# Output stores of 32, 64 or 96 rows in a kernel that fuses a Fourier mixing layer and a SoLU MLP

## The chip, the cores and the metric

The kernel runs on one core of one Trainium2 chip. The metric is the device time of one execution in microseconds (us).

## What is computed

`x` holds 8 batches of S = 3136 tokens with D = 256 channels. The first half filters along the tokens in the frequency domain, the second half is an MLP with a softmax-weighted activation and a norm. `moe_...` names are passed to the second function without the prefix.

```python
def _attn_ref(x, w_r, w_i, b_r, b_i):
    X = np.fft.rfft(x, axis=1)
    Xr, Xi = X.real, X.imag
    Yr = Xr @ w_r - Xi @ w_i + b_r
    Yi = Xr @ w_i + Xi @ w_r + b_i
    # soft threshold by 0.01 on Yr and Yi
    Y = Yr + 1j * Yi
    return np.fft.irfft(Y, n=x.shape[1], axis=1)

def _moe_ref(x, w_in, w_out, g_ln):     # x: 25088 x 256, w_in: 256 x 1024, w_out: 1024 x 256
    h = x @ w_in
    sm = softmax(h)
    solu = h * sm
    ln = (solu - mean(solu)) / sqrt(var(solu) + 1e-6) * g_ln
    return ln @ w_out
```

## The kernel before, in words

**The transform.** S = 98 x 32: a token has the number n1 * 32 + n2 with n1 below N1 = 98 and n2 below N2 = 32. Forward, `fwd1` does the 98-point part (matmuls with `fa`), its result goes to HBM (`s1`), `fwd2` does the 32-point part (`fb`), `mix` applies the weights and the threshold, `inv1` (`gb`) goes back along the 32 and stores `zout` to HBM (`s2`), the last piece as `zs`. `inv2` does the inverse 98-point part for one group of G2 = 4 values of n2: it loads `zt` from `s2`, and its matmuls with `ia` leave 4 x 98 tokens in a PSUM bank, for each half `eh` of the channels one bank. So the tokens of a batch leave the transform in the order n2, n1, not in that of the output.

**The ring.** ACT casts a bank to float16 (`ring_hi`), DVE writes what the cast lost (`ring_lo`). Both are rings of R = 8 tiles of 128 tokens; a group of 392 tokens that reaches the end of the ring is evicted in two pieces.

**The MLP.** It goes in tiles of 128 tokens of the ring, 49 for a pair of batches. `moe_head` does the first matmul (`ph`, 12 matmuls of 512 columns), the exponentials and sums; `moe_turn` casts the activations to `lh` and `ll`, transposes both by DMA into `th` and `tl` and works out the norm's factor `r`; `moe_tail` does the second matmul (`po`, 16 matmuls with `th`, 8 with `tl`), scales on ACT into `o` (two buffers) and stores it. A tile's rows are consecutive in (n2, n1), so one store can only cover the rows of one n2, whose distance in the output is 32 rows of 1 KB: a tile of 128 rows is cut wherever n2 changes, at places that move from tile to tile. This is the loop at the end of `moe_tail`:

```python
        n2, n1 = divmod(jj, N1)
        n = min(N1 - n1, (t + 1) * P - j)
        nc.sync.dma_start(out_v[2 * bp + bb, n2, n1 : n1 + n], o[p0 : p0 + n])
```

The 25th tile of a pair (t = 24) holds the last 64 tokens of the first batch and the first 64 of the second; `h_scale` makes it a scale factor out of two.

**The order.** Nothing is issued as it is written. Each operation is recorded by `Plan.take` with a key; `Plan.order` then lays all of them out by list scheduling over the five engines with its own durations: it takes, on the engine that can start first, the ready operation with the lowest key, and tile buffers are given out in the order of their first users' keys. `Plan.issue` emits the result, so all instructions carry line 342, and the trace is read by tile names. All DMAs are issued by SP, in that one order. Keys count tiles: tile n of batch b has the key `first + n`; `inv2` of a group has a key 2 below the tile that first needs it; `front_b` (fwd2, mix, inv1 of batch b + 1) has keys that begin at `first` and are spread over the batch's tiles, `front_a` (fwd1 of batch b + 2) at `first + 6`.

Of the kernel before, what the change touches and what calls it, by code (L numbers as in the profile page):

```python
# [15 lines left out]
F16 = mybir.dt.float16  # L16
U32 = mybir.dt.uint32
AF = mybir.ActivationFunctionType
ALU = mybir.AluOpType
# [5 lines left out]
S, N1, N2 = 3136, 98, 32  # L25
# [7 lines left out]
S_SCALE, B_SCALE, Z_SCALE, X_SCALE = 2.0**-7, 2.0**-5, 2.0**-11, 2.0**-11  # L33

LOW = 2.0**11
# [416 lines left out]
def fft_mix_solu_kernel(ctx: ExitStack, tc, x, w_r, w_i, b_r, b_i, w_in, w_out, g_ln, fa, fbf, fsf, iaf, fa16, fb, fs, gb, gs, ia, out):  # L452
    nc = Plan(tc.nc)
    B, _, D = x.shape
    FF = w_in.shape[1]
    P = 128
    ND = D // P
# [5 lines left out]
    out_v = out.rearrange("(b n1 n2) e -> b n2 n1 e", b=B, n1=N1)  # L463
# [4 lines left out]
    fp = Pool(ctx.enter_context(tc.tile_pool(name="fp", bufs=2)), 2)  # L468
# [60 lines left out]
    peaks, scales = {}, {}  # L529
# [132 lines left out]
    NU = Q // 2 + 1  # L662
# [165 lines left out]


    G2 = 4  # L830
    R = 8 * P
    ring_hi = const.tile([P, ND, R], F16, name="ring_hi")
    ring_lo = const.tile([P, ND, R], F16, name="ring_lo")

    def inv2(b, g):
        if b >= PLAIN_Z:
            zt = fp.tile([P, G2, 2, D], F16, name="zt", bufs=2)[:N1]
            nc.sync.dma_start(zt.rearrange("c n t d -> c (n t d)"), s2[b][:, g * G2 * 2 * D : (g + 1) * G2 * 2 * D])
        else:
            zt = fp.tile([P, G2, D], F32, name="zt", bufs=2)[:N1]  # L840
            nc.sync.dma_start(zt.rearrange("c n d -> c (n d)"), s2[b][:, g * G2 * D : (g + 1) * G2 * D])
        j0 = (b * S + g * G2 * N1) % R
        n = G2 * N1
        first = min(n, R - j0)
        for eh in range(ND):
            pa = banks.tile("pf")
            nc.reserve(*(ring[:, eh, to : to + z - a] for ring in (ring_hi, ring_lo) for a, z, to in ((0, first, j0), (first, n, 0)) if z > a))
            with nc.together():
                for i in range(G2):
                    es = slice(eh * P, (eh + 1) * P)  # L850
                    if b < PLAIN_Z:
                        nc.tensor.matmul(pa[:, i * N1 : (i + 1) * N1], zt[:, i, es], iaf_s, start=True, stop=True)
                        continue
                    for k, (t, j) in enumerate(((0, 0), (0, 1), (1, 2))):
                        nc.tensor.matmul(pa[:, i * N1 : (i + 1) * N1], zt[:, i, t, es], ia_s[:, j], start=k == 0, stop=k == 2)
            for a, z, to in ((0, first, j0), (first, n, 0)):
                if a == z:
                    continue
                hi, lo = (ring[:, eh, to : to + z - a] for ring in (ring_hi, ring_lo))
                nc.scalar.activation(hi, pa[:, a:z], AF.Copy, scale=X_SCALE)  # L860
                nc.vector.scalar_tensor_tensor(lo, hi, -LOW, pa[:, a:z], ALU.mult, ALU.add)


    def h_scale(k):

        b0, b1 = (2 * k[0] + (k[1] * P + j) // S for j in (0, P - 1))
        if b0 == b1:
            return scales[b0]["h"]
        hs = sp.tile([P, 1], F32, name="hs", bufs=2)
        half = S % P  # L870
        nc.vector.tensor_copy(hs[:half], scales[b0]["h"][:half])
        nc.vector.tensor_copy(hs[half:], scales[b1]["h"][half:])
        return hs

    def moe_head(k):
        j = (2 * k[0] * S + k[1] * P) % R
        hi, lo = ring_hi[:, :, j : j + P], ring_lo[:, :, j : j + P]
        down = h_scale(k)
        ph, nm = [], []
        for h in range(2):  # L880
            cs = slice(h * HF, (h + 1) * HF)
            p = banks.tile("ph")
            n = 0
            with nc.together():
                for dh in range(ND):
                    for lh, rh in ((hi, win_hi), (hi, win_lo), (lo, win_low)):
                        nc.tensor.matmul(p, lh[:, dh], rh[:, dh, cs], start=n == 0, stop=n == 3 * ND - 1)
                        n += 1
            m = sp.tile([P, 1], F32, name="nm")
            nc.vector.tensor_reduce(m, p, AX.X, ALU.max, negate=True)  # L890
            ph.append(p)
            nm.append(m)
        m = sp.tile([P, 1], F32, name="m")
        nc.vector.tensor_scalar(m, nm[0], nm[1], down, ALU.min, ALU.mult)

        c = sp.tile([P, 1], F32, name="c")
        nc.vector.tensor_scalar(c.bitcast(U32), m.bitcast(U32), 0x7FFFFFFF, None, ALU.bitwise_and)
        nc.vector.tensor_scalar(c, c, 1.0, 2.0**-13, ALU.max, ALU.mult)
        nc.vector.reciprocal(c, c)
        ch = sp.tile([P, 1], F32, name="ch")  # L900
        nc.vector.tensor_scalar(ch, c, down, None, ALU.mult)
        u = mp.tile([P, FF], F32, name="u", bufs=4)
        se = [sp.tile([P, 1], F32, name=f"se{h}") for h in range(2)]
        su = [sp.tile([P, 1], F32, name=f"su{h}") for h in range(2)]
        for h in range(2):
            cs = slice(h * HF, (h + 1) * HF)
            nc.scalar.activation(u[:, cs], ph[h], AF.Exp, bias=m, scale=down, accum_out=se[h])
            nc.vector.scalar_tensor_tensor(u[:, cs], ph[h], ch, u[:, cs], ALU.mult, ALU.mult, accum_out=su[h])


        total = sp.tile([P, 1], F32, name="total")
        nc.gpsimd.tensor_tensor(total, su[0], su[1], op=ALU.add)
        nc.gpsimd.tensor_tensor(se[0], se[0], se[1], op=ALU.add)
        a = sp.tile([P, 1], F32, name="a")
        nc.gpsimd.tensor_scalar(a, se[0], 1e-9, c, ALU.add, ALU.mult)
        nc.gpsimd.tensor_tensor(a, a, a, op=ALU.mult)
        return k, u, total, a
# [21 lines left out]
    def moe_tail(k, parts, r):  # L939
        th, tl = parts  # L940
        po = banks.tile("po")
        n = 0
        for part, halves in ((th, 2), (tl, 1)):
            with nc.together():
                for f in range(NF):
                    for j in range(halves):
                        nc.tensor.matmul(po[:, :D], part[:, f], wout[:, f, j], start=n == 0, stop=n == 3 * NF - 1)
                        n += 1
        o = mp.tile([P, D], F32, name="o", bufs=2)
        nc.scalar.activation(o, po[:, :D], AF.Copy, scale=r)  # L950
        bp, t = k
        j = t * P
        while j < (t + 1) * P:
            bb, jj = divmod(j, S)
            n2, n1 = divmod(jj, N1)
            n = min(N1 - n1, (t + 1) * P - j)
            p0 = j - t * P
            nc.sync.dma_start(out_v[2 * bp + bb, n2, n1 : n1 + n], o[p0 : p0 + n])
            j += n

# [168 lines left out]
    def front_b(b, key, step):  # L1131

        lag = 4 if b == 0 else 3
        for n in range(NU + lag):
            nc.key = key + n * step
            for fn, u in ((fwd2, n), (mix, n - 1)):
                if 0 <= u < NU:
                    fn(b, u)
            u = n - lag
            if u == NU - 1 or 0 <= u < NU and b == 0:  # L1140

                inv1(b, u, u + 1)
            elif 0 < u < NU and u % 2:
                inv1(b, u - 1, u + 1)
# [18 lines left out]
    heads, turned = [], []  # L1163
    first = 0
    for b in range(B):
        tiles = range(0, 24) if b % 2 == 0 else range(24, 49)
        L = len(tiles)
        if b == 0:
            front_a(1, -40, 0.5)
        if b + 2 < B:  # L1170
            front_a(b + 2, first + 6, (L - 6) / 17)
        if b + 1 < B:
            front_b(b + 1, first + (6 if b == 0 else 0), (L - (8 if b == 0 else 2)) / (NU + 3))
        groups = 0
        for n, t in enumerate(tiles):
            need = min((t + 1) * P - (b % 2) * S, S)
            while groups < N2 // G2 and groups * G2 * N1 < need:
                nc.key = first + n - 2
                inv2(b, groups)
                groups += 1  # L1180
            nc.key = first + n
            heads.append(moe_head((b // 2, t)))
            nc.key = first + n + 0.5
            turned.append(moe_turn(*heads.pop(0)))
            nc.key = first + n + 1
            moe_tail(*turned.pop(0))
        while groups < N2 // G2:
            inv2(b, groups)
            groups += 1
        first += L  # L1190
    nc.issue(tc)

# [23 lines left out]
```

## Time and profile before

| | us |
|---|---|
| median of 3 runs (lowest, highest) | 1635.44 (1632.08, 1636.81) |
| the profiled execution | 1638.51 |
| its span on the core | 1636.7 |
| PE matmul busy | 1586.2 |
| DVE, ACT, POOL busy | 1317.3, 1234.6, 1129.3 |
| mean granted TensorE clock | 0.986 |

The profile shows one execution. Engines: PE matmuls, PEld weight loads beside them, DVE, ACT, POOL; SPq is SP's queue, which issues the DMAs. Idle time before an instruction is put down to what released it, as `<-DMA th<-lh`: the transposing DMA that writes `th` from `lh`. A DMA's own row on SPq is the time of its issue, not of its transfer.

### The profile page before, as it was taken

The numbers are of one execution on the slowest core, as the hardware profiler recorded it, in microseconds if no ns is written. First come the engines' busy times: TensorE is split into PE (matmuls) and PEld (weight loads), VectorE is DVE, ScalarE is ACT, GpSimd is POOL, SyncE is SP. The second block draws the span as 40 slices with busy tenths as digits, with TensorE's granted clock in tenths as the row PEclk, the third lists the DMA queues.
The fourth block names the chain that finished last, engine by engine and source line by source line (L and its number), as shares of the span: only waits on it lengthen the run. The fifth ranks groups of instructions, "written<-read, shape, count | busy, mean of one in ns | idle before, by whom it ended". The sixth has DMA issues, their size and how long they took to land.

```text
span 1636.7 us, 37871 instructions
## 1 busy us (share of the span) xinstructions
PE 1586.2 (97%) x13040; PEld 1127.8 (69%) x13040; DVE 1317.3 (80%) x3343; ACT 1234.6 (75%) x2496; POOL 1129.3 (69%) x1889
## 2 busy tenths in 40 slices
PE   6979999999999999999999999999999999999998
PEld 3545877676775787668766677766877677676675
DVE  4778779985888867997799977899689877777774
ACT  4667678885788767887678867788678876678786
POOL 0656777676875687768766687766887677776775
PEclk8989999999999999999999999999999999999999
DMA  8868966997669977899758996699767977669776
GB/s 249 274 223 205 194 149 155 229 207 146 151 151 233 214 152 133 189 249 192 162 102 191 251 209 132 134 234 243 162 134 158 191 165 145 119 137 144 150 130 106
DMA packets 532258, 290.23 MB, mean 177 GB/s; under 512 B 425978, under 2 KB 502300, under 8 KB 532064
## 3 DMA queue, kind: packets, MB, share of 16 engines
q1 hardware_dynamic: 532064, 287.81, 80.9%
q8 instruction: 102, 1.67, 0.4%
q14 instruction: 92, 0.75, 0.1%
HBM read 107.89 MB, written 77.07 MB: 113 GB/s over the span
## 4 chain that ended last, share of the span: by engine, by line
PE 78%; DMA 8%; DVE 5%; ACT 3%; POOL 2%; issue 2%; SPq 0%; DVEq 0%; ACTq 0%; POOLq 0%
PE po L342 26%; PE ph L342 24%; PE pf L342 23%; PE pb L342 4%; DMA th<-lh 4%; DMA tl<-ll 3%; DVE u L342 1%; POOL ll L342 1%; ACT junk L342 1%; DVE xl L342 1%; ACT lh L342 1%; DVE nm L342 1%; ACT u L342 0%; DMA zt<-s 0%; DVE av L342 0%
## 5 line engine op out<-in xcount | busy, mean ns | idle before, releaser
L342 POOL TENSOR_TENSOR ll<-u,lh 128x1024 f16<-128x1024 f32 x196 | 427.2, 2180 | 116.0 <-ACT lh L342 110.0
L342 PE MATMUL po<-wout,th 128*128 128x256 f16 x3136 | 375.3, 273 | 10.6 <-DMA th<-lh 9.2
L342 PEld LDWEIGHTS <-th 128*128 128x128 f16 x3136 | 303.8, 98 | 74.5 <-DMA th<-lh 15.8
L342 ACT ACTIVATE u<-ph,m,hsb 128x512 f32<-128x512 f32 x384 | 296.1, 776 | 50.5 <-DVE m L342 46.9
L342 DVE TENSOR_REDUCE nm<-ph 128x1 f32<-128x512 f32 x392 | 265.0, 684 | 82.3 <-PE ph L342 80.7
L342 DVE SCALAR_TENSOR_TENSOR u<-ph,ch,u 128x512 f32<-128x512 f32 x392 | 281.6, 747 | 31.1 <-ACT u L342 20.0
L342 PE MATMUL ph<-win_hi,ring_hi 128*128 128x512 f16 x784 | 298.2, 380 | 1.3 <-DVE ring_lo L342 0.8
L342 PE MATMUL ph<-win_low,ring_lo 128*128 128x512 f16 x784 | 297.8, 380 | 0.0
L342 PE MATMUL ph<-win_lo,ring_hi 128*128 128x512 f16 x784 | 297.8, 380 | 0.0
L342 ACT CAST lh<-u 128x1024 f16<-128x1024 f32 x196 | 205.3, 1047 | 64.2 <-DVE u L342 57.2
L342 PEld LDWEIGHTS <-ring_hi 128*128 128x128 f16 x1568 | 150.3, 98 | 142.7 <-issue 5.9
L342 ACT ACTIVATE junk<-u,total 128x1024 bf16<-128x1024 f32 x196 | 226.0, 1153 | 13.1 <-POOL total L342 12.8
L342 PE MATMUL po<-wout,tl 128*128 128x256 f16 x1568 | 204.2, 273 | 6.3 <-DMA tl<-ll 6.3
L342 PEld LDWEIGHTS <-tl 128*128 128x128 f16 x1568 | 150.4, 98 | 39.8 <-DMA tl<-ll 8.6
L342 POOL TENSOR_TENSOR y<-yt,yc 128x512 f32<-128x512 f32 (+1 forms) x104 | 133.0, 1279 | 61.0 <-ACT yt L342 32.7
L342 POOL TENSOR_TENSOR yl<-y,yh 128x512 f16<-128x512 f32 (+1 forms) x104 | 127.2, 1224 | 47.6 <-ACT yh L342 47.0
L342 PE MATMUL pf<-w_hi,Xh 128*128 128x256 f16 (+1 forms) x546 | 149.2, 273 | 0.0
L342 PE MATMUL pf<-w_hi,Xl 128*128 128x256 f16 (+1 forms) x546 | 148.8, 273 | 0.0
L342 PE MATMUL pf<-w_lo,Xh 128*128 128x256 f16 (+1 forms) x546 | 148.8, 273 | 0.0
L342 ACT ACTIVATE o<-po,r 128x256 f32<-128x256 f32 x196 | 92.6, 473 | 72.0 <-PE po L342 53.8
L342 PEld LDWEIGHTS <-ring_lo 128*128 128x128 f16 x784 | 76.7, 98 | 93.8 <-DVE ring_lo L342 0.8
L342 PEld LDWEIGHTS <-Xh 128*128 128x128 f16 (+1 forms) x1196 | 114.2, 99 | 27.7 <-issue 3.7
(189 smaller groups left out, 2851.0 us busy)
## 6 DMA issues: line engine op xcount, KB each, us to landing
xt<-in_x_dram SPq DMA_DIRECT2D x108, 392.0 KB
zt<-s SPq DMA_DIRECT2D x56, 392.0 KB
s<-zout SPq DMA_DIRECT2D x42, 512.0 KB
s<-av SPq DMA_DIRECT2D x48, 392.0 KB
bin<-s SPq DMA_DIRECT2D x36, 512.0 KB
out_dram<-o SPq DMA_DIRECT2D x64, 98.0 KB
bin<-s1f SPq DMA_DIRECT2D x12, 512.0 KB
s1f<-av SPq DMA_DIRECT2D x10, 392.0 KB
```

Source lines behind the costliest of these rows:

```text
L342: getattr(engine, name)(*args, **kw)
```

## The change

A tile now takes tokens of 96-token runs: for each n2 the ring gets the first N96 = 96 of the 98 tokens, so a batch has 24 tiles of 128 = 96 + 32, 64 + 64 or 32 + 96 rows. The last two tokens of each n2, 64 for a batch, go to a tile of their own, `last_hi` and `last_lo`, one buffer each, that two batches fill; it is the pair's 25th tile of the second batch (t is None), and in the output its rows are two runs of 64. The ring has R = 2 x 4 x 96 tokens, two groups; a bank is evicted into the ring and into `last` by two instructions on each engine. `front_b` of batches 2 to 7 begins two keys earlier, with a smaller step, and `inv2` of a group stands 3 keys below the tile that needs it.

```diff
     G2 = 4
-    R = 8 * P
+    N96 = N1 - N1 % 16
+    R = 2 * G2 * N96
...
-        j0 = (b * S + g * G2 * N1) % R
-        n = G2 * N1
-        first = min(n, R - j0)
+        j0 = (b * N2 + g * G2) * N96 % R
+        if g == 0 and b % 2 == 0:
+            lasts[b // 2] = [fp.tile([P, ND, 2, N1 - N96, N2], F16, name=f"last_{part}", bufs=1) for part in ("hi", "lo")]
...
+            to = [
+                (
+                    ring[:, eh, j0 : j0 + G2 * N96].rearrange("p (i n) -> p i n", n=N96),
+                    last[:, eh, b % 2, :, g * G2 : (g + 1) * G2].rearrange("p n i -> p i n"),
+                )
+                for ring, last in zip((ring_hi, ring_lo), lasts[b // 2])
+            ]
+            nc.reserve(*to[0], *to[1])
...
-            for a, z, to in ((0, first, j0), (first, n, 0)):
-                if a == z:
-                    continue
-                hi, lo = (ring[:, eh, to : to + z - a] for ring in (ring_hi, ring_lo))
-                nc.scalar.activation(hi, pa[:, a:z], AF.Copy, scale=X_SCALE)
-                nc.vector.scalar_tensor_tensor(lo, hi, -LOW, pa[:, a:z], ALU.mult, ALU.add)
+            pv = pa[:, : G2 * N1].rearrange("p (i n) -> p i n", n=N1)
+            for hi, lo, ns in zip(*to, (slice(0, N96), slice(N96, N1))):
+                nc.scalar.activation(hi, pv[:, :, ns], AF.Copy, scale=X_SCALE)
+                nc.vector.scalar_tensor_tensor(lo, hi, -LOW, pv[:, :, ns], ALU.mult, ALU.add)
...
     def moe_head(k):
+        b, t = k
+        if t is None:
+            hi, lo = (part.rearrange("p e b n i -> p e (b n i)") for part in lasts.pop(b // 2))
+        else:
+            j = (b * N2 * N96 + t * P) % R
...
+        b, t = k
+        if t is None:
+            for i in range(2):
+                nc.sync.dma_start(out[(b + i) * S - P // 2 : (b + i) * S], o[i * P // 2 : (i + 1) * P // 2])
+            return
+        p = 0
+        while p < P:
+            n2, n1 = divmod(t * P + p, N96)
+            n = min(N96 - n1, P - p)
+            nc.sync.dma_start(out_v[b, n2, n1 : n1 + n], o[p : p + n])
+            p += n
...
-            front_b(b + 1, first + (6 if b == 0 else 0), (L - (8 if b == 0 else 2)) / (NU + 3))
+            front_b(b + 1, first + (6 if b == 0 else -2), (L - (8 if b == 0 else 4)) / (NU + 3))
...
-            need = min((t + 1) * P - (b % 2) * S, S)
-            while groups < N2 // G2 and groups * G2 * N1 < need:
-                nc.key = first + n - 2
+            while groups < N2 // G2 and groups * G2 * N96 <= n * P:
+                nc.key = first + n - 3
                 inv2(b, groups)
                 groups += 1
```

How the order moves, at three places. First SP in batch 1, before: stores of `o` (rows x 256 channels), between transposes.

```order
L342 DMA bin<-s_3464 128x4x512
L342 DMA_TRANSPOSE tl<-ll 128x8x128
L342 DMA out_dram<-o 34x256
L342 DMA out_dram<-o 94x256
L342 DMA_TRANSPOSE th<-lh 128x8x128
L342 DMA out_dram<-o 4x256
L342 DMA out_dram<-o 98x256
L342 DMA out_dram<-o 26x256
L342 DMA_TRANSPOSE tl<-ll 128x8x128
```

And SP in the same batch with the change.

```order
L342 DMA_TRANSPOSE tl<-ll 128x8x128
L342 DMA out_dram<-o 64x256 x2
L342 DMA_TRANSPOSE th<-lh 128x8x128
L342 DMA out_dram<-o 32x256
L342 DMA out_dram<-o 96x256
L342 DMA_TRANSPOSE th<-lh 128x8x128
L342 DMA_TRANSPOSE tl<-ll 128x8x128
L342 DMA out_dram<-o 96x256
L342 DMA out_dram<-o 32x256
```

Transposes and stores follow each other as before; the stores' row counts are others, and there are two for each tile.

Second, SP where batch 2's transform ends, before: `zs` is its last store, `zt` its first loads for `inv2` (`s_5493` is its buffer in HBM, `s_7051` that of batch 3's fwd1).

```order
L342 DMA s_5493<-zs 64x512
L342 DMA_TRANSPOSE th<-lh 128x8x128
L342 DMA xt<-in_x_dram 128x784
L342 DMA_TRANSPOSE tl<-ll 128x8x128
L342 DMA s_7051<-av 98x2048
L342 DMA xt<-in_x_dram 128x784
L342 DMA out_dram<-o 52x256
L342 DMA out_dram<-o 76x256
L342 DMA zt<-s_5493 98x2048 x2
```

The same place with the change (`s_5517` and `s_7224` are the same two buffers).

```order
L342 DMA s_5517<-zs 64x512
L342 DMA xt<-in_x_dram 98x1024
L342 DMA s_7224<-av 98x2048
L342 DMA_TRANSPOSE th<-lh 128x8x128
L342 DMA out_dram<-o 64x256 x2
L342 DMA zt<-s_5517 98x2048
L342 DMA xt<-in_x_dram 98x1024
L342 DMA zt<-s_5517 98x2048
L342 DMA_TRANSPOSE tl<-ll 128x8x128
```

The end of the transform has moved: before, it is row 357 of SP's 1200 and the next load of `zt` comes 12 rows after the first; now it is row 309 of 1082 and the next load of `zt` comes 37 rows after the first.

Third, DVE at the first groups of batch 2, before: `ring_lo` is the eviction, one instruction for a half that doesn't wrap.

```order
L342 TENSOR_REDUCE nm<-ph 128x1 x2
L342 TENSOR_SCALAR yc<-yt,sc 128x512
L342 TENSOR_SCALAR m<-nm,hsb 128x1
L342 SCALAR_TENSOR_TENSOR ring_lo<-ring_hi,pf 128x392
L342 TENSOR_SCALAR c<-m 128x1
L342 SCALAR_TENSOR_TENSOR ring_lo<-ring_hi,pf 128x392
L342 TENSOR_SCALAR c<-c 128x1
```

And DVE there with the change.

```order
L342 RECIPROCAL c<-c 128x1
L342 SCALAR_TENSOR_TENSOR ring_lo<-ring_hi,pf 128x384
L342 SCALAR_TENSOR_TENSOR last_lo<-last_hi,pf 128x4x2
L342 SCALAR_TENSOR_TENSOR ring_lo<-ring_hi,pf 128x384
L342 SCALAR_TENSOR_TENSOR last_lo<-last_hi,pf 128x4x2
L342 TENSOR_SCALAR ch<-c,hs 128x1
L342 TENSOR_REDUCE peaks<-xt 128x1
```

Each half is now evicted by a large and a small instruction.

## Rows read from the trace of the kernel before

**Rows 1.** The page's busy times: us, share of the span, instructions.
```profile
PE 1586.2 (97%) x13040; PEld 1127.8 (69%) x13040; DVE 1317.3 (80%) x3343; ACT 1234.6 (75%) x2496; POOL 1129.3 (69%) x1889
```
**Rows 2.** Busy by stretches: stretch, length, engines' busy us, clock, DMA share, GB/s.
```profile
164.00:1610.00 1446.00, 1428.62 (x12150) 1031.99 (x12150) 1190.47 (x3051) 1118.82 (x2269) 1039.72 (x1766) 1.00 0.82 172
1620.00:1637.00 17.00, 9.18 (x66) 6.62 (x63) 2.39 (x9) 5.31 (x12) 5.70 (x12) 0.87 0.49 92
519.90:526.70 6.80, 5.32 (x52) 4.50 (x53) 3.94 (x9) 4.05 (x9) 3.56 (x7) 0.50 1.18 231
```
**Rows 3.** Waits of PE from 164 to 1610: us in total, times, longest.
```profile
PE po L342 <- DMA th<-lh: 7.3, 9, 1.6
PE po L342 <- DMA tl<-ll: 4.6, 5, 2.3
PE pf L342 <- DMA zt<-s: 4.1, 1, 4.1
PE ph L342 <- DVE ring_lo L342: 0.8, 1, 0.8
```
**Rows 4.** Timeline of PE: start, length, instruction, [idle before it, releaser].
```profile
193.13 1.05 PE L342 MATMUL po<-wout,tl 128*128 128x256 f16 x8 [0.41 <-DMA tl<-ll]
...
368.27 1.92 PE L342 MATMUL po<-wout,th 128*128 128x256 f16 x16 [0.27 <-DMA th<-lh]
...
375.81 0.94 PE L342 MATMUL po<-wout,th 128*128 128x256 f16 x7 [1.62 <-DMA th<-lh]
...
390.00 1.05 PE L342 MATMUL po<-wout,tl 128*128 128x256 f16 x8 [0.95 <-DMA tl<-ll]
...
1371.12 1.05 PE L342 MATMUL po<-wout,tl 128*128 128x256 f16 x8 [2.34 <-DMA tl<-ll]
```
**Rows 5.** Timeline of SP's queue, ahead of those: start, length of the issue.
```profile
183.37 0.73 SPq L342 DMA_DIRECT2D out_dram<-o  x2
...
362.74 2.26 SPq L342 DMA_DIRECT2D out_dram<-o  x2
365.10 1.27 SPq L342 DMA_TRANSPOSE th<-lh  x1
...
368.43 0.79 SPq L342 DMA_DIRECT2D out_dram<-o  x2
369.27 2.39 SPq L342 DMA_TRANSPOSE th<-lh  x1
...
383.57 1.00 SPq L342 DMA_DIRECT2D out_dram<-o  x2
...
1362.07 0.60 SPq L342 DMA_DIRECT2D out_dram<-o  x2
```
**Rows 6.** The chain in order of time: start, length, from issue to the released work.
```profile
184.20 8.89 DMA tl<-ll
...
384.68 5.27 DMA tl<-ll
...
1363.21 7.87 DMA tl<-ll
```
**Rows 7.** Timeline of ACT at 374.8.
```profile
374.81 0.47 ACT L342 ACTIVATE o<-po,r 128x256 f32<-128x256 f32 x1 [2.08 <-DMA out_dram<-o]
```
**Rows 8.** Issues of the output stores: ns shortest/median/longest, first and last start.
```profile
L342 SPq DMA_DIRECT2D out_dram<-o x448: 237/343/1852, 150.1 to 1633.9; - x150
```
**Rows 9.** Timeline of SP and PE at batch 2's first inverse groups.
```profile
513.37 1.90 SPq L342 DMA_DIRECT2D zt<-s  x2
...
521.38 4.10 PE L342 MATMUL pf<-ia_s,zt 98*128 98x98 f16 x48 [4.07 <-DMA zt<-s]
```
**Rows 10.** DVE's ring evictions: busy us, mean ns, idle before; then ns shortest/median/longest.
```profile
L342 DVE SCALAR_TENSOR_TENSOR ring_lo<-ring_hi,pf 128x392 f16<-128x392 f16 (+32 forms) x176 | 74.2, 443 | 8.8 <-ACT ring_hi L342 8.2
L342 DVE SCALAR_TENSOR_TENSOR ring_lo<-ring_hi,pf x176: 152/519/564, 118.3 to 1596.4; 128x392 f16<-128x392 f16 x80, 128x240 f16<-128x240 f16 x2, 128x152 f16<-128x152 f16 x2, 128x88 f16<-128x88 f16 x2
```
**Rows 11.** The chain: forty tail matmuls in a row.
```profile
1156.87 4.37 PE po L342 x40
```

More of the change, by code (lines that the diff above doesn't have):

```diff
@@ L830, in fft_mix_solu_kernel @@
     G2 = 4
-    R = 8 * P
+    N96 = N1 - N1 % 16
+    R = 2 * G2 * N96
     ring_hi = const.tile([P, ND, R], F16, name="ring_hi")
     ring_lo = const.tile([P, ND, R], F16, name="ring_lo")
+    lasts = {}
     def inv2(b, g):
@@ L841, in inv2 @@
             nc.sync.dma_start(zt.rearrange("c n d -> c (n d)"), s2[b][:, g * G2 * D : (g + 1) * G2 * D])
-        j0 = (b * S + g * G2 * N1) % R
-        n = G2 * N1
-        first = min(n, R - j0)
+        j0 = (b * N2 + g * G2) * N96 % R
+        if g == 0 and b % 2 == 0:
+            lasts[b // 2] = [fp.tile([P, ND, 2, N1 - N96, N2], F16, name=f"last_{part}", bufs=1) for part in ("hi", "lo")]
         for eh in range(ND):
             pa = banks.tile("pf")
-            nc.reserve(*(ring[:, eh, to : to + z - a] for ring in (ring_hi, ring_lo) for a, z, to in ((0, first, j0), (first, n, 0)) if z > a))
+            to = [
[6 more added lines that the diff above has]
+            nc.reserve(*to[0], *to[1])
             with nc.together():
@@ L855, in inv2 @@
                         nc.tensor.matmul(pa[:, i * N1 : (i + 1) * N1], zt[:, i, t, es], ia_s[:, j], start=k == 0, stop=k == 2)
-            for a, z, to in ((0, first, j0), (first, n, 0)):
-                if a == z:
-                    continue
-                hi, lo = (ring[:, eh, to : to + z - a] for ring in (ring_hi, ring_lo))
-                nc.scalar.activation(hi, pa[:, a:z], AF.Copy, scale=X_SCALE)
-                nc.vector.scalar_tensor_tensor(lo, hi, -LOW, pa[:, a:z], ALU.mult, ALU.add)
+            pv = pa[:, : G2 * N1].rearrange("p (i n) -> p i n", n=N1)
+            for hi, lo, ns in zip(*to, (slice(0, N96), slice(N96, N1))):
+                nc.scalar.activation(hi, pv[:, :, ns], AF.Copy, scale=X_SCALE)
+                nc.vector.scalar_tensor_tensor(lo, hi, -LOW, pv[:, :, ns], ALU.mult, ALU.add)
     def h_scale(k):
-        b0, b1 = (2 * k[0] + (k[1] * P + j) // S for j in (0, P - 1))
-        if b0 == b1:
-            return scales[b0]["h"]
+        b, t = k
+        if t is not None:
+            return scales[b]["h"]
         hs = sp.tile([P, 1], F32, name="hs", bufs=2)
-        half = S % P
-        nc.vector.tensor_copy(hs[:half], scales[b0]["h"][:half])
-        nc.vector.tensor_copy(hs[half:], scales[b1]["h"][half:])
+        half = P // 2
+        nc.vector.tensor_copy(hs[:half], scales[b - 1]["h"][:half])
+        nc.vector.tensor_copy(hs[half:], scales[b]["h"][half:])
         return hs
     def moe_head(k):
-        j = (2 * k[0] * S + k[1] * P) % R
-        hi, lo = ring_hi[:, :, j : j + P], ring_lo[:, :, j : j + P]
+        b, t = k
[3 more added lines that the diff above has]
+            j = (b * N2 * N96 + t * P) % R
+            hi, lo = ring_hi[:, :, j : j + P], ring_lo[:, :, j : j + P]
         down = h_scale(k)
@@ L950, in moe_tail @@
         nc.scalar.activation(o, po[:, :D], AF.Copy, scale=r)
[L951 to L959, printed above, removed]
+        b, t = k
+        if t is None:
[8 more added lines that the diff above has]
+            p += n
     pw = banks.tile("po")
@@ L1165, in fft_mix_solu_kernel @@
     for b in range(B):
-        tiles = range(0, 24) if b % 2 == 0 else range(24, 49)
-        L = len(tiles)
+        L = 24 + b % 2
         if b == 0:
@@ L1172, in fft_mix_solu_kernel @@
         if b + 1 < B:
-            front_b(b + 1, first + (6 if b == 0 else 0), (L - (8 if b == 0 else 2)) / (NU + 3))
+            front_b(b + 1, first + (6 if b == 0 else -2), (L - (8 if b == 0 else 4)) / (NU + 3))
         groups = 0
-        for n, t in enumerate(tiles):
-            need = min((t + 1) * P - (b % 2) * S, S)
-            while groups < N2 // G2 and groups * G2 * N1 < need:
-                nc.key = first + n - 2
+        for n in range(L):
+            while groups < N2 // G2 and groups * G2 * N96 <= n * P:
+                nc.key = first + n - 3
                 inv2(b, groups)
@@ L1181, in fft_mix_solu_kernel @@
             nc.key = first + n
-            heads.append(moe_head((b // 2, t)))
+            heads.append(moe_head((b, n if n < 24 else None)))
             nc.key = first + n + 0.5
@@ L1186, in fft_mix_solu_kernel @@
             moe_tail(*turned.pop(0))
-        while groups < N2 // G2:
-            inv2(b, groups)
-            groups += 1
         first += L
```

## The prediction

> **What bounds the kernel now.** I read the page first, for the busy shares [rows 1]: PE is busy for 97% of the span, DVE for 80%, ACT for 75%, POOL for 69%. A share of 97% leaves little to win, so the question is where the other 50 us lie. The table by stretches answers it [rows 2]. From 164 us, when the start is over, to 1610 us, PE is busy for 1428.6 of 1446.0 us: 17.4 us idle in the whole steady part. The last 17 us hold 7.8 us idle, the pipeline running empty behind the last tile, and the rest of the idle time is in the first 164 us. The third row is a stretch in which the granted clock was 0.50, the lower of the two levels (1.2 GHz): 6.8 us long, so about 3.4 us of matmul time were lost there. Nothing that the change does to stores can give back more than 17.4 + 3.4 = 20.8 us, apart from the start and the end, which it leaves alone: neither the work before the first tile nor the last tiles' chain gets shorter.
>
> Then the waits of PE in that steady part [rows 3]: 7.3 us for the transposed tile `th`, 4.6 us for `tl`, 4.1 us for one load of `zt`, 0.8 us for an eviction to the ring. So nearly all of PE's idle time ends with a DMA, and the bound is PE with a few late transfers on top. To see why a transfer was late I looked at single waits in order of time [rows 4] and at what SP had issued just ahead of each [rows 5]. The wait of 1.62 us at 375.8 is for a transpose issued at 369.27, 6.5 us before; in front of it stands the pair of stores of 368.43, which the order shows to have 34 and 94 rows. Four microseconds earlier a transpose behind two stores of 64 rows (362.74) was issued at 365.10 and used at 368.27, 3.2 us later. The other long ones have the same neighbours: 0.41 us at 193.1 behind stores of 46 and 82 rows (183.37), 0.95 us at 390.0 behind 42 and 86 rows (383.57), 2.34 us at 1371.1 behind 46 and 82 rows (1362.07). The chain of waits gives the transposes themselves from issue to use [rows 6]: 8.9, 5.3 and 7.9 us. And one row tells of such a store directly [rows 7]: at 374.81 ACT had to wait 2.08 us for a buffer of `o` until a store of the pair of 368.43 had landed, over 6 us after its issue.
>
> The Trainium skill, "DMA: Bandwidth & Descriptors", section "Why a DMA increments its semaphore by 16 and not by 1", has a rule for this: a DMA runs on the largest number of engines up to 16 that divides its slowest dimension. By it 34, 46, 82, 86 and 94 rows run on 2 engines, 98 on 14, and 32, 64 and 96 on 16. That agrees with which pairs stand ahead of the late transposes; no row of the profile counts the engines of one store.
>
> **The change, part by part.**
>
> *Stores.* 448 stores of 2 to 98 rows [rows 8] become 392 of 32, 64 or 96. They carry the same bytes. On SP that is 56 issues fewer, at a median of 0.343 us some 19 us of queue time; SP is not what PE waits for, so I cost this at 0. What I take as gained are the four waits that stand behind odd pairs: 0.41 + 1.62 + 0.95 + 2.34 = 5.3 us. The bounds: 0, if those transposes were late for the loads around them, and 11.9 us, if all waits for `th` and `tl` go [rows 3]. I take 5.3, because the others (6.6 us) stand behind loads that the change keeps.
>
> *Keys of the front and of the inverse.* For batches 2 to 7 the transform starts two tile numbers earlier and its steps are closer together, and the inverse step's key is one lower. In the order, the store that ends batch 2's transform and its first two loads of `zt` then stand far ahead of their use: the next load of that kind, which needs one of the two buffers back, comes 37 SP rows after the first of them, where it was 12. Before, this was the place of the longest wait in the steady part [rows 9]: two loads issued from 513.37, the first used at 521.38, PE idle for 4.07 us, and the clock at 0.50 right after. With the load done ahead of time both go: 4.07 + 3.4 = 7.5 us. Lower bound of the gain: 0, if another late load does the same elsewhere; upper bound 7.5, there was only one.
>
> *Evictions.* Each of 128 banks of the inverse step (64 groups, two halves) is now emptied by two ACT and two DVE instructions: one for 384 tokens, one for 8. Before there were 176 on each, since a group could wrap around the ring. DVE's 176 took 443 ns on average [rows 10], 78.0 us in sum. Now: 128 small ones at the shortest duration seen, 152 ns, are 19.5 us, and 128 large ones at no more than the longest, 564 ns, are 72.2 us: 91.7 us, up to 13.7 us more work on DVE, and about as much on ACT, which has more room [rows 1]. PE waited for an eviction for 0.8 us in all [rows 3]. The cover is the idle fifth of DVE; where DVE is full, the extra work would show as PE waiting for `ring_lo`. Bounds: 0 and 13.7 us; I take 2 us, near the row of 0.8.
>
> *Ring and last tile.* The ring shrinks from 8 tiles to 6, two groups of 3 tiles each. A group may then be written when the last tile of the group two before it has been read, with three tiles of matmul work still ahead of its own use: no wait for PE. The tile of last tokens is new: it has one buffer, so the first group of a new pair of batches (batches 2, 4, 6) can't be written until the heads of the pair's closing tile have read it. In the order the first two groups of batch 2 stand right behind that head and 16 tail matmuls, and the next head follows after 8 more. What lies between is little, and the evictions have to fit in. Nothing before shows such a hold. Its bounds: 0, when the second group's matmuls and the tails cover the eviction, and the worst wait for data on this step, 4.07 us plus 3.4 us of low clock, each of three times. The nearest row is the wait for `ring_lo`, 0.8 us, so I take 1 us each, 3 us.
>
> **Sum.** -5.3 - 7.5 + 2 + 3 = -7.8 us. Against the profiled execution's own time, 1638.5 us (span 1636.7), that is 1630.7 us. This execution lies 3.1 us above the median of the runs, 1635.4, so for the median I expect **1627.6 us**. A measurement here can tell a difference of about 0.3%, 4.9 us, from none: faster means below 1630.5, slower above 1640.3.
>
> **Rivals.**
>
> *No change that shows.* The transposes are late because the DMA engines are full: their share is 0.82 over the whole steady part and above 1 in the stretch of the long wait [rows 2]. Then other row counts only shift the same bytes about, late transfers find new places, and of the 7.5 us some 3 are left: 1635.4 - 3 + 2 = 1634 us, within 0.3%. For it: the 6.6 us of waits behind loads. Against it: the pair 3.2 us and 6.5 us, four microseconds apart, and the store that took over 6 us. [...]
>
> *Slower: a hold at the change of pair.* The single buffer of last tokens makes head, inverse, eviction and next head stand in a row at batches 2, 4 and 6. If PE then idles as at 521 us, each costs 4.07 + 3.4 = 7.5 us, 22.4 us in all; with the stores' gain and the extra evictions 1635.4 + 22.4 - 7.5 - 5.3 + 2 = 1647 us. It decides for slower from about (4.9 + 7.5 + 5.3 - 2) / 3 = 5.2 us per pair on. For it: the buffer count, and DVE and ACT in order with transforms of the next batch in the same stretch. Against it: 16 tail matmuls ahead of the two groups and 8 behind them, 24 x 109 ns = 2.6 us of work that needs neither buffer (40 of them take 4.37 us [rows 11]), and the second group beside the first one's eviction.
>
> *More.* All late transfers vanish, and with them the low clock: 1635.4 - 20.8 = 1614.6 us, if the odd stores were also what made the transposes behind loads late.
>
> **Chances and range.** The forecast (1624 to 1630) gets 0.47, more gain (down to 1615) 0.13, no change that shows 0.24, the hold 0.16. So faster 0.60, same 0.24, slower 0.16. The range 1616 to 1642 leaves out half of the hold and the last step of the best case.
>
> **What would show it.** Right: 392 stores, none of the waits of PE over 1 us behind a pair of stores, `th` and `tl` waits of PE in the steady part near 6 us; no wait for `zt` of 4 us and no stretch at 0.50 between 164 us and the tail; waits for `ring_lo` and `ring_hi` together under 5 us. Wrong: if waits for `th` and `tl` stay at 12 us or grow, the stores were not their cause; if PE idles for several microseconds between the last tile of a pair and the first of the next, the hold has come; if PE's idle time falls and the span does not, something other than idle time grew, and the step that I have missed is in PE's own work.

## The result, and the profile after

| | before | with the change |
|---|---|---|
| median of 4 runs (lowest, highest), us | 1635.16 (1632.08, 1636.81) | 1616.44 (1616.38, 1616.65) |
| span of the profiled execution, us | 1636.7 | 1614.9 |
| mean granted TensorE clock | 0.986 | 0.990 |

The ratio is 0.9888, 95% interval 0.9871 to 0.9905: faster by 18.7 us, where 7.8 were forecast. The same kernel on another chip (e9 below) took 1617.79 against 1631.32 us: 0.9912, interval 0.9896 to 0.9927, 13.5 us. The sign was right, the size was not.

The busy times, as in [rows 1]:

```profile
PE 1577.4 (98%) x13040; PEld 1126.1 (70%) x13040; DVE 1326.1 (82%) x3423; ACT 1238.8 (77%) x2576; POOL 1123.6 (70%) x1889
```

The stretches, as in [rows 2]: the steady part (here to 1588 us, so that both kernels can be cut alike), the 6.8 us that ran at the lower clock before, the start's slowest stretch and the end. A line `...` stands where rows of the view are left out.

```profile
164.00:1588.00 1424.00, 1420.62 (x12125) 1029.20 (x12123) 1196.62 (x3116) 1119.21 (x2333) 1033.00 (x1767) 1.00 0.79 175
...
519.90:526.70 6.80, 6.80 (x41) 3.84 (x40) 6.80 (x21) 4.41 (x11) 4.04 (x10) 1.00 1.10 265
...
82.00:123.00 41.00, 32.05 (x182) 19.02 (x177) 32.27 (x66) 26.51 (x59) 21.63 (x15) 0.85 0.68 223
...
1598.20:1615.00 16.80, 9.88 (x80) 7.21 (x77) 3.82 (x13) 7.59 (x14) 7.31 (x14) 1.00 0.55 101
```

The same two stretches of the kernel before:

```profile
164.00:1588.00 1424.00, 1406.62 (x11981) 1016.75 (x11981) 1174.31 (x3004) 1100.96 (x2235) 1024.01 (x1734) 1.00 0.82 173
...
82.00:123.00 41.00, 32.65 (x174) 19.01 (x174) 32.27 (x65) 26.07 (x53) 20.69 (x14) 0.80 0.69 223
```

PE's idle time in the steady part fell from 1424.00 - 1406.62 = 17.4 us to 3.4 us: 14.0 us. The stretch at 0.50 has gone; PE was busy for 5.32 of its 6.8 us [rows 2], so half of that, 2.7 us, was lost there. That is 16.7 of the 21.8 us by which the spans differ. The other 5.1 us lie outside: the clock from 82 to 123 us was 0.85 instead of 0.80 (about 2 us), and in the last 17 us it was 1.00 instead of 0.87, with 6.9 us idle instead of 7.8. The change's repeat (e9) had 0.83 in the first of these stretches and 0.86 in its last 17 us, so that part varies from execution to execution; I claim nothing from it.

The waits of PE in the steady part, as in [rows 3]:

```profile
PE pf L342 <- DVE u L342: 1.5, 1, 1.5
PE po L342 <- DVE c L342: 1.3, 2, 0.7
PE pf L342 <- DVE c L342: 0.4, 1, 0.4
PE ph L342 <- DVE u L342: 0.2, 1, 0.2
```

Not one of them ends with a DMA: 7.3 us for `th`, 4.6 for `tl` and 4.1 for `zt` are all gone. What is left waits for DVE: 3.4 us. The stores, as in [rows 8], and the queue that moves their bytes (packets, MB, share of the span of 16 engines), with the change:

```profile
L342 SPq DMA_DIRECT2D out_dram<-o x392: 316/486/1679, 152.8 to 1611.9; - x196
...
q1 hardware_dynamic: 533728, 287.82, 78.5%
```

And that queue before:

```profile
q1 hardware_dynamic: 532064, 287.81, 80.9%
```

The packets of the same 287.8 MB took 0.809 x 1636.7 = 1324 us of each of the 16 engines before and 0.785 x 1614.9 = 1268 us now (engine time below). So this queue, which carries loads, transposes and stores, moves the same bytes in less engine time; it's not the amount of data that changed.

### The profile page after: what moved, and what is told of

It reads as the page before. It is cut to its first block, busy times and chain, and to the rows that moved or that the text cites. A ratio compares the mean times of both kernels' runs of the same rounds, so it can differ in the third digit from the quotient of the medians.

```text
span 1614.9 us, 38042 instructions
## 1 busy us (share of the span) xinstructions
PE 1577.4 (98%) x13040; PEld 1126.1 (70%) x13040; DVE 1326.1 (82%) x3423; ACT 1238.8 (77%) x2576; POOL 1123.6 (70%) x1889
## 4 chain that ended last, share of the span: by engine, by line
PE 92%; DVE 3%; ACT 2%; DMA 1%; issue 1%; POOL 0%; SPq 0%; DVEq 0%; ACTq 0%; POOLq 0%
PE po L342 31%; PE ph L342 30%; PE pf L342 27%; PE pb L342 4%; DVE u L342 1%; DVE xl L342 1%; DVE nm L342 1%; DMA zt<-s2f 0%; ACT u L342 0%; DMA s2f<-zs 0%; ACT junk L342 0%; DMA bin<-s1f 0%; DMA s1f<-tl 0%; DVE av L342 0%; DMA th<-lh 0%
## 5 line engine op out<-in xcount | busy, mean ns | idle before, releaser
L342 DVE SCALAR_TENSOR_TENSOR u<-ph,ch,u 128x512 f32<-128x512 f32 x392 | 281.5, 747 | 23.1 <-ACT u L342 13.7
L342 PE MATMUL ph<-win_hi,ring_hi 128*128 128x512 f16 x768 | 291.9, 380 | 0.2 <-DVE u L342 0.2
L342 PE MATMUL ph<-win_lo,ring_hi 128*128 128x512 f16 x768 | 291.5, 380 | 0.0
L342 PE MATMUL ph<-win_low,ring_lo 128*128 128x512 f16 x768 | 291.3, 379 | 0.0
L342 PEld LDWEIGHTS <-ring_hi 128*128 128x128 f16 x1536 | 146.8, 98 | 140.5 <-issue 6.5
L342 POOL TENSOR_TENSOR yl<-y,yh 128x512 f16<-128x512 f32 (+1 forms) x104 | 122.3, 1178 | 40.3 <-ACT yh L342 39.3
```

Source lines behind the costliest of these rows:

```text
L342: getattr(engine, name)(*args, **kw)
```

## The experiments

Each kernel was timed with the kernel before on the same chip. The median of the kernel before was 1631.86 us for e1 to e4, 1632.4 for e5 to e8, 1631.32 for e9 to e12 and 1630.76 for e13 to e15. Unless said otherwise waits are PE's between 164 and 1588 us. Edits of a store's rows stand where an operation is emitted, behind the ordering, so that the order of all instructions stays that of the kernel edited; the line number moves with the lines added. Where an edit takes rows from a store, these rows are missing in the output.

### e1 and e2: the change's stores with other row counts

```diff
+                    if name == "dma_start" and isinstance(args[1], View) and args[1].tile.kw["name"] == "o":
+                        n = args[1].shape[0]
+                        n = {96: 94, 64: 62}.get(n, n)      # e2: {96: 90, 64: 60}
+                        args = (args[0][:n], args[1][:n])
```

> The changed kernel with the same order, but each store of 96 rows writes only 94 and each of 64 only 62 (the last two rows of these stores are left out of the output). Theory A, the row counts of the stores made the transposes late: 264 of 392 stores now have counts whose largest divisor up to 16 is 2, against 72 of 448 in the kernel before, so PE's waits for th and tl in the steady part come back and exceed the 11.9 us of the kernel before, and the time is 1628 us or more. Theory B, the new order of the work alone made the waits go: they stay near 0 and the time is 1616 us, within 2.

> The changed kernel with the same order, but stores of 96 rows write 90 and stores of 64 rows 60 (the last 6 or 4 rows of them are left out of the output). 90 and 60 are no multiples of 16 but are divided by 15. Theory A in the form of the largest divisor: no waits, 1616 us within 2. Theory A in the form that only multiples of 16 are quick: waits for th and tl of 5 us or more, 1621 us or more. Theory B: 1616 us within 2.

Measured: e1 1689.25 us, ratio 1.0332 (1.029 to 1.0374); e2 1617.56 us, ratio 0.9896 (0.9858 to 0.9933), the time of the change itself. In e1, 264 of 392 stores have 94 or 62 rows. Its longest waits, steady part and queue:

```profile
PE po L346 <- DMA th<-lh: 24.3, 20, 2.4
PE po L346 <- DMA tl<-ll: 19.8, 18, 3.4
PE pf L346 <- DMA bin<-s: 2.8, 2, 1.8
...
164.00:1588.00 1424.00, 1373.56 (x11631) 983.73 (x11630) 1148.16 (x2968) 1069.68 (x2227) 987.18 (x1667) 0.99 0.88 168
...
q1 hardware_dynamic: 529504, 287.26, 86.7%
```

Fewer bytes than the change moves, and the engines are busy for longer: 0.867 x 1687.2 = 1463 us each, 195 us more than with the change, or 195 x 16 / 264 = 11.8 us of engine time for each store with two rows less, if all of it is put down to these stores. PE's steady part idles for 50.4 us. One place from the chain of waits (start, length):

```profile
326.25 6.33 DMA tl<-ll
332.57 8.36 DMA th<-lh
...
340.98 1.92 PE po L346 x16
```

and what SP issued ahead of the second of them:

```profile
329.13 0.89 SPq L346 DMA_DIRECT2D out_dram<-o  x2
330.11 2.38 SPq L346 DMA_DIRECT2D s<-av  x2
332.57 3.23 SPq L346 DMA_TRANSPOSE th<-lh  x1
```

Between the stores and the transpose stand two stores of `av`. In the trace of before I would have called this transpose "behind loads and other stores", as I did with 6.6 us of waits. In e2, whose stores have 90 and 60 rows, such waits are nearly absent:

```profile
PE po L346 <- DMA th<-lh: 1.5, 1, 1.5
...
PE po L346 <- DMA tl<-ll: 0.8, 1, 0.8
```

So a row count needn't be a multiple of 16. What 96, 90, 64 and 60 share against 94 and 62 is a divisor of 15 or 16; the largest divisor up to 16 of 94 and of 62 is 2. From here on an odd store is one of more than 16 rows whose largest divisor up to 16 is 4 or less, and a clean one has a larger one.

### e3 and e14: the order of before, with its stores cut

e3 cuts the 96 odd ones of the 448 stores, e14 every store of more than 16 rows, to the next lower multiple of 16; nothing else of the kernel before is touched.

```diff
+                    if name == "dma_start" and isinstance(args[1], View) and args[1].tile.kw["name"] == "o":
+                        n = args[1].shape[0]
+                        if max(k for k in range(1, 17) if n % k == 0) <= 4 and n > 16:    # e14: if n > 16:
+                            n -= n % 16
+                        args = (args[0][:n], args[1][:n])
```

> The kernel before with its own order, but its 96 stores whose row count has no divisor from 5 to 16 (34, 38, 46, 58, 62, 68, 74, 76, 82, 86, 92, 94 rows) are cut to the next lower multiple of 16 (2 to 14 rows of each are left out of the output, 848 of 25088 in all). Theory A: PE's waits for th and tl in the steady part fall from 11.9 us to 6.6 us or less, and the time to 1624 to 1630 us. Theory B: waits and time as before, 1635 us within 3.

> The kernel before with its own order, with every store of more than 16 rows cut to a multiple of 16 (the rest of its rows left out of the output). If only stores with a largest divisor up to 4 cost something: as with the 96 cut, 1622 us within 3. If those with 5 to 15 do too: 1619 us or less.

Measured: e3 1621.76 us, 0.9927 (0.9901 to 0.9954), 10.1 us faster than before; e14 1622.61 us, 0.9953 (0.9936 to 0.9969), 8.2 us. The two agree, so largest divisors between 9 and 15 cost nothing that shows (no store of more than 16 rows has one of 5 to 8). They agree though e14 moves 285.4 MB and e3 286.95, so the bytes left out aren't what makes e3 faster. The waits and the queue of e3:

```profile
PE po L347 <- DMA th<-lh: 3.2, 4, 1.3
PE ph L347 <- ACT ring_hi L347: 1.7, 2, 1.4
PE ph L347 <- DVE ring_lo L347: 0.8, 1, 0.8
PE po L347 <- DMA tl<-ll: 0.4, 1, 0.4
...
q1 hardware_dynamic: 532512, 286.95, 77.5%
```

`th` and `tl` together fell from 11.9 to 3.6 us, and the wait for `zt` isn't there at all, though no key was changed. Of the four waits that the prediction named, 5.3 us, one of 0.45 us is left (at 1358 us); of the 6.6 us behind loads about half is, at the same three places as before (324, 821 and 835 us in e3). PE now waits 1.7 us for `ring_hi`. The timeline at the place of [rows 9], in e3:

```profile
505.73 1.51 SPq L347 DMA_DIRECT2D out_dram<-o  x2
...
507.29 1.01 SPq L347 DMA_DIRECT2D zt<-s  x2
...
512.80 2.32 PE L347 MATMUL pf<-ia_s,zt 98*128 98x98 f16 x48
```

The two stores just ahead are those of 52 and 76 rows, of which e3 sends 52 and 64. The loads are issued as late as before in the order, and used 5.5 us after their issue without a wait; before it was 8.0 us (513.37 to 521.38). No stretch at 0.50 follows. So with clean stores this late `zt` goes without an earlier key. Which of the cuts did it is not shown: one store at this place was cut, and 95 others, earlier and later, which shift what is in flight here.

### e4, e5, e12 and e13: the two keys by themselves

e4 is the kernel before with the two keys; e5 and e12 are the change with the keys of before, on two chips; e13 is e3 with the two keys.

```diff
-            front_b(b + 1, first + (6 if b == 0 else 0), (L - (8 if b == 0 else 2)) / (NU + 3))
+            front_b(b + 1, first + (6 if b == 0 else -2), (L - (8 if b == 0 else 4)) / (NU + 3))
...
-                nc.key = first + n - 2
+                nc.key = first + n - 3
```

> The kernel before with its tiles and stores, but with the two keys of the change (the transform of batches 2 to 7 begins two keys earlier with the smaller step, the inverse step's key 3 below its tile). Theory A: the wait for zt and the low clock behind it go, 7.5 us, the waits for th and tl stay near 12 us: about 1628 us. Theory B, the order did it all: waits for th, tl and zt under 4 us together, 1617 to 1621 us.

> The changed kernel with the two keys of the kernel before (transform from the batch's first tile on with the larger step, inverse step 2 below its tile); tiles and stores are those of the change. Theory A, the stores alone did it: waits of PE for th, tl and zt in the steady part stay under 4 us, 1614 to 1620 us. Theory C, the keys carry the 7.5 us that the prediction gave them: about 1624 us.

> The changed kernel with the two keys of the kernel before, once more, beside the change on one chip. Theory A alone: within 3 us of the change. Theory C: 5 to 10 us slower than the change, with the wait for zt at the start of batch 5 in its profile.

> The kernel before with its tiles, with its 96 odd stores cut as in the third experiment (848 rows of the output left out) and with the two keys of the change. If stores and keys make the whole gain: within 3 us of the change, 1613 to 1620 us. If the new tiles themselves carry a part: 1621 us or more, as with the cut alone.

Measured: e4 1628.74 us, 0.9985 (0.9968 to 1.0003), not told apart from no change; e5 1624.51 us, 0.9952 (0.9935 to 0.9969); e12 1624.53 us, 0.9957 (0.9941 to 0.9973), which is 6.7 us above the change itself on the same chip (e9); e13 1625.16 us, 0.997 (0.9957 to 0.9983), no better than e14 on the same chip (1622.61). In e4 a wait for `zt` is still the longest, at 321 us, where batch 1's inverse begins, and the clock behind it falls to 0.50 (322 to 324 us):

```profile
PE pf L342 <- DMA zt<-s: 2.6, 1, 2.6
PE po L342 <- DMA tl<-ll: 2.3, 3, 1.1
PE pf L342 <- DVE u L342: 1.9, 3, 0.9
...
PE po L342 <- DMA th<-lh: 0.5, 2, 0.3
```

`th` and `tl` together are 2.8 us here, where theory A had 12: with all 96 odd stores in place, the order that the keys make takes 9.1 us off these waits. So an odd store makes a transpose late in one order and not in another. The time hardly follows, since PE is idle for 11.5 us of the steady part even so, for the `zt` of batch 1 and for DVE. In e13 the same place has two waits in a row, at 319 and at 322 us, and a clock of 0.50 from 323 to 326 us, with clean stores:

```profile
PE ph L347 <- ACT ring_hi L347: 2.0, 1, 2.0
...
PE pf L347 <- DMA zt<-s: 1.2, 1, 1.2
```

In e5 the late load comes back too, three batches later than in [rows 9], and the stretch behind it has a clock of 0.75 (timeline of PE, then the table by stretches):

```profile
1094.17 3.10 PE L342 MATMUL pf<-ia_s,zt 98*128 98x98 f16 x48 [2.84 <-DMA zt<-s]
...
1094.20:1101.00 6.80, 6.80 (x70) 5.45 (x71) 5.26 (x16) 4.69 (x13) 3.88 (x8) 0.75 0.97 308
```

In e12 the wait at this place is 2.6 us, and the clock stays at 1.00. So the keys are worth 6.7 us in the new tiles (the intervals of e12 and e9 don't overlap), and nothing that shows in the old ones, with odd stores or without. An earlier key is not worth a fixed sum: in these traces it moves the place of the latest load, from batch 2 to batch 1 in the old tiles.

e13's two rivals were that stores and keys make the whole gain, within 3 us of the change, or that the new tiles carry a part, 1621 us or more. It came out as the second: clean stores and keys in the old tiles gain 5.6 us, not 13.5.

### e6, e7 and e11: last tile and evictions

e6 gives the tile of last tokens two buffers; e7 issues each small eviction twice, e11 four times.

```diff
-...name=f"last_{part}", bufs=1)
+...name=f"last_{part}", bufs=2)
```

```diff
+                    twice = op.engine in ("scalar", "vector") and args[0].tile.kw["name"].startswith("last_")
-                    getattr(engine, name)(*args, **kw)
+                    for _ in range(1 + twice):              # e11: 1 + 3 * twice
+                        getattr(engine, name)(*args, **kw)
```

> The changed kernel with two buffers for the tile of last tokens, so that the first group of a new pair needn't wait for the pair's closing head. The prediction's price of the hold, 1 us for each of 3 pairs: 3 us faster, 1613 us. If the hold costs nothing: 1616 us within 2.

> The changed kernel with each small eviction of last tokens issued twice, on ACT and on DVE: 128 more instructions on each, some 20 us of work on DVE and 23 on ACT, in the same order. The prediction's price, 2 us for 13.7 us: 3 us slower, 1619 us. If DVE's and ACT's idle time hides it: 1616 us within 1. If it lies on the path where DVE is full: up to 20 us slower.

> The changed kernel with each small eviction issued four times on ACT and DVE, 384 more instructions on each, some 60 us more work on DVE and 70 on ACT. If the idle time of both hides it: no more than 3 us over the change. If it shows where DVE is full, as a third of the span is: 10 to 30 us more.

Measured: e6 1620.43 us, 0.9927 (0.9912 to 0.9942), no gain from the second buffer; since the buffer also changes the order, it can't say more than that the hold costs nothing that shows, and none of the change's own waits above is for it. e7 1622.14 us, 0.9935 (0.992 to 0.9949), some 4 us above the change's results on other chips, with an interval that overlaps e9's, and 1.7 us above e6 on its own chip. e11 1668.22 us, 1.0222 (1.0201 to 1.0242), 50 us above the change on the same chip, where 30 were the most expected. The evictions with the change, against [rows 10] (forms apart: busy us, mean ns, idle before):

```profile
L342 DVE SCALAR_TENSOR_TENSOR ring_lo<-ring_hi,pf 128x384 f16<-128x384 f16 x128 | 70.0, 548 | 4.3 <-ACT last_hi L342 2.9 <-ACT ring_hi L342 0.3 <-PE pf L342 0.3
...
L342 DVE SCALAR_TENSOR_TENSOR last_lo<-last_hi,pf 128x8 f16<-128x8 f16 x128 | 23.3, 182 | 0.5 <-ACT last_hi L342 0.5
```

They are 93.3 us of DVE instead of 78.0: 15.3 us more, beside an upper bound of 13.7, because a small one takes 182 ns where I took 152. In e11 the 512 small ones take 96.7 us of DVE and 106.3 us of ACT instead of 23.3 and 27.7: 73 and 79 us more, and 50 us reach the end:

```profile
PE pf L344 <- DVE u L344: 6.1, 6, 1.7
PE ph L344 <- DVE u L344: 4.4, 5, 1.4
PE pf L344 <- DVE Xl L344: 3.9, 8, 0.8
...
164.00:1588.00 1424.00, 1385.79 (x11741) 994.45 (x11740) 1220.88 (x3356) 1144.57 (x2605) 1003.03 (x1692) 1.00 0.76 170
```

With DVE at 1220.88 / 1424.00 = 86% in this part, PE waits for `u`, the step between `ph` and the transposes. ACT had as much added and is busy for 80% there; which of the two costs the 50 us was not separated. The idle fifth of DVE is a cover for a little work, not for 73 us on it and 79 on ACT.

### e8, e10 and e15: how many odd stores, and where

e8 gives every fourth of the change's 264 large stores 94 or 62 rows (66 of them), e10 every second (132); e15 only the stores of 64 rows, which go in pairs (136).

```diff
+                        seen += n > 32
+                        if seen % 4 == 0:                   # e10: % 2; e15: without this, {64: 62}
+                            n = {96: 94, 64: 62}.get(n, n)
```

> The changed kernel with the same order, but every fourth store of 96 or 64 rows, 66 of 392, writes 94 or 62 (two rows of each of these are left out of the output): as many stores with a largest divisor of 2 as the kernel before has (72). Theory A: waits for th and tl in the steady part between 5 and 15 us, 1622 to 1634 us. If the waits need many such stores, or just the places that the old order had: under 4 us, 1617 to 1619 us.

> The changed kernel with the same order, with every second store of 96 or 64 rows, 132 of 392, at 94 or 62 (two rows of each left out of the output). Theory A with a price for each store: half of what 264 of them cost, about 36 us, so some 1652 us, with waits for th and tl near 22 us in the steady part. If only stores that come in pairs or crowds cost: less than a third of that, under 1640 us.

> The changed kernel with the same order, where the two stores of each tile of 64 + 64 rows write 62 + 62 (136 stores, two rows of each left out of the output), and those of 96 and 32 stay. As many as in the tenth experiment, but always two behind each other. If single stores cost little and pairs much: 1632 us or more, with waits for th and tl of 10 us or more in the steady part. If only the number counts: 1624 us within 3.

Measured: e8 1622.58 us, 0.9941 (0.9924 to 0.9958), 2 us above e6 on the same chip, so its odd stores cost nothing that shows for certain; e10 1623.75 us, 0.9953 (0.9936 to 0.997), 6 us above the change on the same chip; e15 1639.77 us, 1.005 (1.0026 to 1.0075), 22 us above the change's 1617.79 on another chip. The waits for `th` and `tl` are 2.4 us in e8, where theory A had 5 to 15, and 1.7 us in e10, where it had 22:

```profile
PE po L349 <- DMA tl<-ll: 1.4, 4, 0.5
...
PE po L349 <- DMA th<-lh: 0.3, 1, 0.3
...
q1 hardware_dynamic: 531616, 287.54, 82.0%
```

That is an engine time of 0.820 x 1620.8 = 1329 us, as much as in the kernel before (1324), which had 11.9 us of these waits. So the engine time by itself doesn't make the transposes late. PE's idle time in the steady part is only 1.3 us more than in e9; where the rest of e10's 6 us lies is open. e15 has the waits:

```profile
PE po L346 <- DMA th<-lh: 9.7, 11, 2.0
PE po L346 <- DMA tl<-ll: 8.6, 8, 2.8
...
q1 hardware_dynamic: 531552, 287.53, 82.7%
```

136 odd stores that always follow one another cost over three times what 132 cost that mostly stand alone. e1's 264 cost 72 us (1689.25 against 1617.56 for e2, on the same chip).

### e9: the change itself on another chip

> The changed kernel once more, beside the three that follow, so that they are compared on one chip. It says how far its time moves from chip to chip: 1616 us within 3.

Measured: 1617.79 us, 0.9912 (0.9896 to 0.9927); waits of 1.5 us for `u`, 1.3 for `c`, 0.5 for `tl`. The gain is 13.5 us here and 18.7 us in the first comparison; the kernel before differs more between the two (1631.32, 1635.16) than the change does (1617.79, 1616.44).

## Why the prediction was wrong in size

**The step that failed** is the term of the stores, "I take 5.3, because the others (6.6 us) stand behind loads that the change keeps". I had counted a wait for the stores only where an odd pair was the last thing ahead of the transpose in SP's order. With the change `th` and `tl` fell by the whole 11.9 us. e3 keeps every load, every key and the whole order, cuts 96 stores, and `th` and `tl` fall by 11.9 - 3.6 = 8.3 us, `zt` by 4.1 us and the low clock with it; the time falls by 10.1 us (e14: 8.2). The four waits named made 4.9 of the 8.3 us; the other 3.4 came from transposes that stand behind loads. Those loads were kept, so the odd stores, several transfers ahead, had a part in these waits too. How they did it is not shown: engine time fell from 1324 to 1257 us in e3, but e10 has 1329 us without late transposes. Nor were the stores needed for it: the keys alone took 9.1 us off the same waits (e4). The gain in the first comparison is near that of the rival "more", to which I gave 0.13 under the condition that the odd stores made the transposes behind loads late as well.

**Keys.** Forecast -7.5 us, of which 3.4 for the low clock; since PE was busy for 5.32 of the 6.8 us and the 1.5 us before are the end of the 4.07 us wait already counted, the two come to 4.07 + 2.7 = 6.8 us. In the new tiles the keys measured -6.7 us (e12 against e9). That the size is near is in part luck: the wait of [rows 9] goes without the keys too (e3), in the old tiles they bring nothing that shows (e4, e13), and the late load that comes back without them in e12 is 2.6 us with no low clock.

**Evictions.** Forecast +2 us, of 0 to 13.7. DVE's work grew by 15.3 us, a little over the bound. What that costs was not measured by itself: e7's 128 more cost 1.7 to 4 us, which the intervals can't tell from nothing. All that PE still waits for in the steady part is DVE, 3.4 us. "The cover is the idle fifth of DVE" holds for such an amount and falls at 384 (e11).

**Ring and last tile.** Forecast +3 us; none was seen. No wait of the change is for `ring_lo`, `ring_hi` or `last_lo`, and a second buffer gains nothing (e6). So the rival of the hold fell, too.

**Sum.** In the profiled executions, against the terms of the forecast: `th` and `tl` -11.9 us (stores, -5.3), `zt` and the low clock -6.8 (keys, -7.5), waits for the ring -1.1, waits for DVE +3.4 (evictions, +2), the hold 0 (+3), the start and the end -5.1 (0): -21.5 us of the 21.8 between the spans. So the term of the stores lacked 6.6 us, the hold was 3 us that didn't come, and some 5 us lie where I had expected nothing and where executions differ. This says which waits went, not which part of the edit took them away. On the chip of e9 and e12 the change without its keys is 6.8 us faster than before, and the keys add 6.7: 13.5 us. In the old tiles clean stores alone gain 8.2 to 10.1 us (e14, e3), but clean stores and keys together only 5.6 (e13), which isn't told apart from e14. The parts don't add up by themselves, so what the new tiles bring beyond clean stores stays open. The first comparison's 18.7 us are 5 us more than e9's; why the kernel before was slower there is open.

**The rivals.** "No change that shows" needed the same bytes to take the same engine time; they don't, and e1 against e2 shows it with the same order and nearly the same bytes. The DMA share above 1 is still there at 520 us (1.10), with PE busy throughout: a full DMA stretch didn't have to be a late transfer.

**What was to show it.** 392 stores, no wait for `zt` of 4 us, no stretch at 0.50 and no waits for the ring: all came. "`th` and `tl` waits near 6 us" was wrong: 0, and 0.5 us in e9.

**Open.** Why the keys gain in the new tiles and not in the old; how much the 15.3 us on DVE cost; and which transfers in flight turn an odd store into a late transpose.

## What to carry to other kernels

Cut tiles so that the row count of every store has a divisor near 16, and avoid above all two stores with a small one in a row: here 94 and 62 rows instead of 96 and 64 cost 72 us for 264 stores, 90 and 60 nothing. When a transfer is late, don't blame the transfer just ahead of it in the queue alone: test by changing the suspected class of transfers everywhere, with the order held fixed. Then test another order with the class kept, since either can take the same wait away (e3, e4). A saving from an earlier key belongs to the whole schedule, so measure it in the version that is to be kept.

## What the runs showed of the hardware that I had not expected

**Divisors, not multiples of 16.** 90 and 60 rows are as good as 96 and 64 (e2), 94 and 62 are not (e1), and largest divisors of 9 to 15 cost nothing that shows (e14 against e3). The Trainium skill, "DMA: Bandwidth & Descriptors", section "Why a DMA increments its semaphore by 16 and not by 1", says that the engine count is the largest number up to 16 that divides the slowest dimension; by it those are 15 against 2 engines, and the runs agree in which counts are cheap. No row here counts the engines of a store.

**The price grows faster than the number.** Above the change: 66 odd stores 2 to 5 us, not told from nothing (e8), 132 spread 6 us (e10), 136 in pairs 22 us (e15), 264 of all kinds 72 us (e1). The added engine time for each odd store grew as well: (0.802 x 1620.5 - 1268) x 16 / 66 = 7.7 us in e8, (1329 - 1268) x 16 / 132 = 7.4 us in e10, (0.827 x 1642.0 - 1268) x 16 / 136 = 10.6 us in e15 and 11.8 us in e1.

**Bytes don't tell a store's time.** e1's stores are smaller than the change's: its queue moves 0.6 MB less and takes 195 us more of each engine.

**A late load can be paid for twice.** In [rows 2] the clock fell to 0.50 right behind PE's idle time of 4.07 us; in e3, where that wait is gone by the stores alone, no such stretch lies between 164 us and the tail. It isn't the stores that decide: in e13, with clean stores, two waits of 1.2 and 2.0 us were followed by a clock of 0.50, and in e12 a wait of 2.6 us wasn't.
